# Raw weights in one ring of six blocks, and another order of the Strassen groups in two runs of a Trainium2 kernel

## The chip, the cores and the metric

The kernel runs on one core of a Trainium2 chip. Five engines with instruction queues of their own work side by side: TensorE (PE, with its weight loads shown apart as PEld), VectorE (DVE), ScalarE (ACT), GpSimd (POOL) and SyncE (SP), whose queue issues most of the DMAs. An instruction starts when those before it on its engine have been issued and the semaphores that it waits for have been raised. The metric is the time of one execution on the device in microseconds (us); lower is better.

## What is computed

Attention with sigmoid weights for 2 batches of 12 heads (448 positions, 64 wide), then a gated MLP behind an RMS norm, then a second MLP, all in FP32 on 896 tokens (cut from the reference):

```
scores = scale * matmul(q, k.T) - log(S)
x = matmul(1 / (1 + exp(-scores)), v)                    # as 896 tokens x 768
xn = x / sqrt(mean(x * x) + 1e-6) * rms_g
h = silu(xn @ w_gate) * (xn @ w_val)                     # 768 -> 1536
y = h @ w_out                                            # 1536 -> 768
h2 = y @ w_in                                            # 768 -> 2048
return (h2 * sigmoid(h2)) @ w_out2                       # 2048 -> 768
```

## The kernel before

**Products.** An FP32 product is three passes of rounded operands (high by high, high by low, low by high). Most matrix products are Strassen runs: seven groups of matmuls on 2x2 blocks, named by the weight side A11, S1, S2, A12, S3, S4 and A22, each 128x128 against 128x448 columns, collecting in PSUM banks x, y, z (L798). Plain products are on L747. ACT *saves* a bank between groups where one bank is used for several (L830, L884, tiles named ..s0 to ..s3), and DVE adds the rest (L836, L891, L978, L1062, L1065). The stages in order of time: attention, g and v (the gated MLP), o0 to o2 (its output, "the layer behind the norm"), i0 to i7 (in the second MLP), e0, e1, e2, e0b, e1b (its output).

**Weights.** They come as 76 slabs of 64-bit words, 52 of 768 KB (six tiles of 128 columns) and 24 of 512 KB (four tiles, the short slabs of the o stages and of some in e). One SP DMA loads a slab into a raw buffer (L239). ACT takes the exponent part out of it (L257, into a buffer named f, or `spare` for single tiles) and turns the other half in place (L265), DVE merges both (L269). Sums and differences of blocks are made in place (L687 to L709), and each *piece* that a group needs is split into a high part on ACT (L245) and a low part on DVE (L248) in a ring of nine. `wraw` is a pool of two buffers of a full slab each, so two slabs are in flight at most, whatever their width.

**What sets the order.** A class `Plan` holds every operation as a job with its engine, cost, dependencies and, where needed, a stock that it takes ("raw", "f", "ring", "alt", "sum"). PE's jobs stand in program order; the others get a due time, counted back from their users by cost, a factor WAIT, an engine's LAG and HOP, and each engine takes the startable job that is due first. That simulated order is what the engines' queues hold. A load is a job of SP that takes "raw", given back by the merge, and counts with LAG["S"] = 4.4 us.

**The o stages.** `mixed` does o0 and o1 with `ahead=True`: first the plain products of the two-bank pairs a and b (o0a, o0b), then the groups in the order A11, S1, S2, A12, S3, S4, A22. Before the groups, ACT saves bank b's first half (tile s3); A11, S2, S3 and A22 go to bank x, S1 and S4 to y, A12 into bank a. Bank pair b is free for the next stage after that save and the addition c11, which follows S3.

Of the kernel before, what the change touches and what calls it, by code (L numbers as in the profile page):

```python
# [22 lines left out]
P = 128  # L23
# [16 lines left out]
LAG = {"A": 0.0481, "D": 0.081, "P": 0.165, "S": 4.4, "G": 5.0}  # L40
HOP = {"A": 0.516, "D": 0.3833, "S": 0.4, "G": 0.5}
# [34 lines left out]
class Plan:  # L76
# [37 lines left out]
    def run(self, busy):  # L114
# [8 lines left out]
        for j in reversed(self.jobs):  # L123
            if j.eng != "P":
                j.due = min([u.due for u in j.users + j.users_of_gift], default=1e9) - WAIT[j.eng] * j.cost - LAG[j.eng] - HOP[j.eng]
# [30 lines left out]
        while left:  # L156
# [6 lines left out]
            while again:  # L163
                again = False
                for e in ("P", "D", "A", "S", "G"):
# [17 lines left out]
                    end = now + j.cost + LAG[e]  # L183
# [14 lines left out]
def tile_attention_two_mlps(  # L198
# [12 lines left out]
    wraw = ctx.enter_context(tc.tile_pool(name="wraw", bufs=2))  # L211
# [23 lines left out]

    def load(s):
        raws[s] = wraw.tile([P, 2 * SLAB], U32, tag="raw", name=f"raw{s}")
        n = 2 * wide(s)
        nc.sync.dma_start(raws[s][:, :n], wd[s].bitcast(U32)[:, :n])  # L239

    def load_next():
        load(order.pop(0))
# [7 lines left out]
    def words(s):  # L250
        return raws[s][:, : 2 * wide(s)].rearrange("p (n two) -> p n two", two=2)
# [329 lines left out]
    plan = Plan({"raw": 0, "f": 1, "ring": RING - 8, "alt": 1, "sum": 1, "ps": 0, "one": 0})  # L581
# [57 lines left out]
    wjob = {}  # L639
# [21 lines left out]
    def weight_mac(macs, act_z, alt=True, early=False):  # L661

        todo = [mac_steps(s, n, act_z, alt, early) for s, n in macs]
        for _ in range(8):
            for t in todo:
                next(t)

    def mac_steps(s, n, act_z, alt, early):
# [24 lines left out]

        s1 = dve(hw, first, m, take=None if inside else "sum")
# [24 lines left out]
        if one:  # L719
            plan.frees("alt" if alt else "f", l1, l2, l4, l5, l6)  # L720
        else:
            if not inside:
                plan.frees("sum", l1, s2)
            plan.frees("f", *[l2, l5] + ([l1] if inside else []))
            plan.frees("alt" if inside else "f", l4, l6)
# [146 lines left out]
    def mixed(  # L872
# [26 lines left out]
        if ahead:  # L899
            bx, by = Banks(f"{name}x"), Banks(f"{name}y")  # L900
            ba, bb = Banks(f"{name}a", True), Banks(f"{name}b", True)
            bz, bv, bu, bw = ba.bank(0), ba.bank(1), bb.bank(0), bb.bank(1)
            done = []
            for k in range(0, n, 2):
                for m, t in enumerate((ba, bb)):
                    i = 2 * k + 2 * m
                    done += product(
                        [t.bank(0), t.bank(1)], w[i : i + 2], keys[k : k + 2], (0, 1), first=k == 0,
                        final=k == n - 2 and m > 0, take="ps" if k == 0 else None, start=t.start if k == 0 else None,
                    )  # L910
            u = save(3, bu, done[-1])
        else:
            bx, by, bz, bw = (Banks(f"{name}{c}") for c in "xyzw")
# [6 lines left out]
        g4 = g(bz, "A12", start=not ahead, stop=ahead, first=None if ahead else bz)  # L920
        if ahead:
            a00 = add(0, bz, [g4, v0], 0, 0)
        g5 = g(bx, "S3", deps=[v2])
        a11 = add(1, bx, [g5, v1])
        if ahead:
            c11 = add(1, bw, [a11], 1, 1)
            bb.read_by(u, c11)
        g6 = g(by, "S4", stop=ahead, deps=[v1])
        if ahead:
            a01 = add(2, by, [g6, v2])  # L930
            c01 = add(2, bv, [a01], 0, 1)
            by.read_by(v1, a01)
            ba.read_by(a00, c01)
        if not ahead:
            p0 = product([bz, by], w[:n], keys, (0, 1), first=False)
        g7 = g(bx, "A22", stop=ahead, deps=[a11])
        if ahead:
            a10 = add(3, bx, [g7, u], 1, 0)
            bx.read_by(a10)
            return  # L940
# [442 lines left out]
    for t in range(3):  # L1383
        dest = lambda m, b, t=t: r2[t]()[:, b, m]
        n = 0 if t < 2 else 3
        macs, plain = [(s + 2, 3), (s + 4, 1)] if t < 2 else [(s, 3), (s + 2, 1)], s + n
# [4 lines left out]
        if t < 2:  # L1391
            weight_mac(macs, ZO)
        macs = [(macs[0][0], range(3)), (macs[1][0], (3,))]
# [184 lines left out]
```

## Time and profile before

| | |
|---|---|
| median of 3 runs | 523.17 us (521.27 to 523.77) |
| profiled execution | 522.38 us |
| its span, first to last instruction | 520.4 us |
| PE busy | 515.3 us (99%) |
| DVE busy | 471.3 us (91%) |
| ACT busy | 380.5 us (73%) |
| granted TensorE clock | 1.00 of full |
| moved by DMA | 70.5 MB |

The profiled execution takes 2.0 us outside the span of its instructions. Busy time is by the hardware's records; matmuls are pipelined, so one's record overlaps the next.

### The profile page before, as it was taken

The page shows a single profiled execution, that of the slowest core. Times are in us where ns is not written, and L with a number is a line of the kernel's source. Part 1 is how long each engine was busy: PE and PEld are TensorE (multiplying, and loading weights), DVE is VectorE, ACT ScalarE, POOL GpSimd, SP SyncE. Part 2 cuts the span into 40 slices and gives each one's busy share as a digit, 9 for nine tenths or more (in the row PEclk, how much of TensorE's full clock was granted, in tenths as well). Part 3 has the DMA queues.
Part 4 walks back from the last instruction along what each step waited for, and adds up shares of the span by engine and source line. Part 5 has one row for each costly group of instructions (what it writes and reads, how often), then busy time and mean ns, then how long its engine had stood idle before and what let it go on. Part 6 is the DMA issues. An engine that isn't in the chain of part 4 may idle for free.

```text
span 520.4 us, 7479 instructions
## 1 busy us (share of the span) xinstructions
PE 515.3 (99%) x2654; PEld 442.7 (85%) x2654; DVE 471.3 (91%) x883; ACT 380.5 (73%) x677; POOL 13.5 (3%) x28
## 2 busy tenths in 40 slices
PE   9999999999999999999999999999999999999996
PEld 4444469999999999999999999999998999999996
DVE  6799999999999888799989989999988899999992
ACT  6876754787888676876777868998888887778730
POOL 0000000000000000000000000000010101111000
PEclk9999999999999999999999999999999999999999
DMA  8774111033332353411442362333355242555531
GB/s 319 276 248 162 62 62 60 1 122 122 121 123 88 103 209 108 162 42 40 163 161 82 125 217 84 122 121 123 135 186 195 97 134 95 169 199 200 187 123 71
DMA packets 18116, 70.51 MB, mean 136 GB/s; under 512 B 2464, under 2 KB 5024, under 8 KB 18080
## 3 DMA queue, kind: packets, MB, share of 16 engines
q1 hardware_dynamic: 16400, 64.32, 35.8%
q0 software_dynamic: 1536, 5.51, 3.1%
q8 instruction: 20, 0.33, 0.3%
q10 hardware_dynamic: 144, 0.23, 0.1%
q14 instruction: 16, 0.13, 0.1%
HBM read 64.54 MB, written 5.51 MB: 135 GB/s over the span
## 4 chain that ended last, share of the span: by engine, by line
PE 99%; DVE 0%; issue 0%
PE av L409 7%; PE sc L382 6%; PE g L747 3%; PE e2S L798 3%; PE v L747 3%; PE e1x L798 2%; PE o2x L798 2%; PE o1x L798 2%; PE e0bx L798 2%; PE o0x L798 2%; PE e2a L798 2%; PE i6x L798 1%; PE g2x L798 1%; PE i7x L798 1%; PE e0x L798 1%; PE e1bx L798 1%
## 5 line engine op out<-in xcount | busy, mean ns | idle before, releaser
L265 ACT ACTIVATE raw<-raw 128x768 int32<-128x768 uint32 (+1 forms) x70 | 57.4, 825 | 12.9 <-DMA raw<-in_w 9.4
L269 DVE SCALAR_TENSOR_TENSOR f<-f,raw 128x768 uint32<-128x768 uint32 (+1 forms) x65 | 58.4, 900 | 7.5 <-ACT f L257 5.9
L245 ACT ACTIVATE w_S<-f 128x384 fp32r<-128x384 f32 (+1 forms) x90 | 44.7, 497 | 23.0 <-DVE f L698 7.7
L257 ACT ACTIVATE f<-raw 128x768 f32<-128x768 f32 (+1 forms) x65 | 55.7, 859 | 4.4 <-DVE w_S L248 2.6
L248 DVE TENSOR_TENSOR w_S<-f,w_S 128x384 fp32r<-128x384 f32 (+1 forms) x90 | 47.3, 526 | 4.7 <-ACT w_S L245 4.3
L391 ACT ACTIVATE a<-sc,logs 128x896 f32<-128x896 f32 x42 | 39.1, 1008 | 15.3 <-PE sc L382 15.3
L245 ACT ACTIVATE w_A<-f 128x384 fp32r<-128x384 f32 (+1 forms) x84 | 41.2, 500 | 7.2 <-PE o2y L747 1.8
L248 DVE TENSOR_TENSOR w_A<-f,w_A 128x384 fp32r<-128x384 f32 (+1 forms) x84 | 43.8, 533 | 1.8 <-ACT w_A L245 1.8
L409 PE MATMUL av<-a,vr 128*64 128x448 f32 (+1 forms) x192 | 35.4, 552 | 0.0
L409 PEld LDWEIGHTS av<-a,vr 128*64 128x64 f32 (+1 forms) x192 | 10.4, 135 | 21.3 <-issue 20.3
L382 PEld LDWEIGHTS sc<-ks 64*128 64x128 f32 x204 | 18.3, 186 | 10.5 <-issue 5.5
L382 PE MATMUL sc<-ks 64*128 64x448 f32 x204 | 24.7, 380 | 0.0
L1131 DVE TENSOR_TENSOR g<-g 128x448 f32<-128x448 f32 x32 | 19.4, 620 | 0.1
L245 ACT ACTIVATE w_S<-s 128x384 fp32r<-128x384 f32 x24 | 12.5, 520 | 6.0 <-PE g L747 3.1
L709 DVE TENSOR_TENSOR f<-f 128x384 f32<-128x384 f32 (+1 forms) x30 | 15.8, 525 | 0.2
L245 ACT ACTIVATE w_A<-spare 128x128 fp32r<-128x128 f32 (+1 forms) x21 | 7.0, 334 | 12.0 <-DVE spare L269 8.7
L747 PE MATMUL v<-x,w 128*128 128x448 f32 x72 | 15.3, 370 | 0.0
L747 PE MATMUL g<-x,w 128*128 128x448 f32 x72 | 15.3, 368 | 0.0
L747 PEld LDWEIGHTS g<-x,w 128*128 128x128 f32 x72 | 13.4, 188 | 1.7 <-issue 0.7
L747 PEld LDWEIGHTS v<-x,w 128*128 128x128 f32 x72 | 13.5, 188 | 1.4 <-issue 0.4
L248 DVE TENSOR_TENSOR w_S<-s,w_S 128x384 fp32r<-128x384 f32 x24 | 13.3, 552 | 0.9 <-ACT w_S L245 0.9
L687 DVE TENSOR_TENSOR s<-f 128x384 f32<-128x384 f32 x24 | 13.3, 554 | 0.3
(1462 smaller groups left out, 1506.3 us busy)
## 6 DMA issues: line engine op xcount, KB each, us to landing
raw<-in_w SPq DMA_DIRECT2D x52, 768.0 KB, 4.4
raw<-in_w SPq DMA_DIRECT2D x24, 512.0 KB, 3.5
kq<-in_kq SPq DMA_DIRECT2D x11, 448.0 KB, 5.5
out_t<-e SPq DMA_DIRECT2D x8, 224.0 KB, 1.9
vr<-in_v SPq DMA_DIRECT2D x6, 256.0 KB, 4.5
vr<-in_v SPq DMA_DIRECT2D x6, 192.0 KB, 2.5
g_4away<-g POOLq DMA_DIRECT2D x4, 224.0 KB, 2.5
g<-g_4away POOLq DMA_DIRECT2D x4, 224.0 KB, 2.9
```

The source lines that it names most:

```text
L245: nc.scalar.activation(dst, src, AF.Copy)
L248: nc.vector.tensor_tensor(dst, src, hi.bitcast(F32), ALU.subtract)
L257: nc.scalar.activation(floats[s], words(s)[:, :, 1].bitcast(F32), AF.Prelu, scale=2.0**-112, alpha=2.0**32)
L265: nc.scalar.activation(z.bitcast(I32), z, AF.Copy, scale=2.0**-29 * (1 - 2.0**-18), bias=-0.5 + 2.9e-5)
L269: nc.vector.scalar_tensor_tensor(fu, fu, 3, words(s)[:, :, 0], ALU.logical_shift_left, ALU.bitwise_or)
L382: nc.tensor.matmul(ps[to, h, :S], k_[:, keys], q_, start=(step == 0), stop=(step == 2 or plain), skip_group_check=True,)
L391: nc.scalar.activation(a, ps[:, :, :S], AF.Sigmoid, bias=logs, scale=D**-0.5)
L409: nc.tensor.matmul(av[n][h * D : (h + 1) * D, :S], vr[i][rows, c, h, :], a[rows, h, :], start=(begun[n] == 1), stop=(begun[n] == KC + 1), ...
L709: s4 = dve(hw, lambda: tt(block(1), block(1), block(0), ALU.subtract), [s2, l3])
L747: nc.tensor.matmul(banks[b](), t[:, jw], act[key](jx, b), start=(first and i == 0 and n_ == 0), stop=(final and i == n - 1 and n_ == 2), s ...
L798: nc.tensor.matmul(ps(), w[:, jw, j * P : (j + 1) * P], book[t][USES[a]][jx], start=(start and i == 0 and n == 0), stop=(stop and i == len ...
L1131: sub = lambda d, a, b: (lambda: tt(d(), a(), b(), ALU.subtract))
```

## The change

The two buffers of `wraw` become one tile `store` of the same size, seen as six blocks. `place(s)` gives slab s the next three blocks (six tiles) or two (four tiles) in the order in which the program names the slabs, and wraps to block 0 where the rest doesn't suffice; it returns the slabs that held those blocks. The load no longer takes "raw": it depends on the merges of these slabs. The lag of a load depends on its width now (2.6 + 0.45 per tile: 5.3 us for six tiles and 4.4 us for four).

In o0 and o1 the groups run in the order A11, A12, S4, S1, S2, A22, S3; S4 collects in the second half of bank a, A22 in the first half of bank b, and tile s3 is saved from bank x behind S3, at the end. `raw_steps` makes the pieces in the matching order, and the single-tile slab of these stages is listed ahead of the two six-tile ones. The number of computing instructions of each kind stays.

```diff
+    store = wraw.tile([P, 4 * SLAB], U32, name="raw")
+    owner, end = [None] * 6, [0]
+    def place(s):
+        n = 2 * wide(s)
+        at = end[0] if end[0] + n <= 4 * SLAB else 0
+        raws[s], end[0] = store[:, at : at + n], at + n
+        over = {}
+        for k in range(at // (4 * P), (at + n) // (4 * P)):
+            over[owner[k]] = True
+            owner[k] = s
+        return over
...
-        r = None if s in LOADED else plan.add("S", 0.4, lambda: load(s), take="raw")
+        over = [] if s in LOADED else place(s)
+        r = None if s in LOADED else plan.add("S", 0.4, lambda: load(s), [merged[u] for u in over if u is not None])
+        if r:
+            r.lag = LOAD + LOAD_TILE * tiles
...
-        return plan.frees("raw", dve(n, lambda: merge(s), [e, z]))
+        merged[s] = dve(n, lambda: merge(s), [e, z])
+        return merged[s]
...
-            u = save(3, bu, done[-1])
+            v0 = save(0, bx, g(bx, "A11", start=True, stop=True, first=bx))
+            a00 = add(0, bz, [g(bz, "A12", stop=True), v0], 0, 0)
+            g6 = g(bv, "S4", stop=True)
+            g2_ = g(by, "S1", start=True, stop=True, first=by)
+            v1 = save(1, by, g2_)
+            g3 = g(bx, "S2", deps=[v0])
+            v2 = save(2, bx, g3)
+            a01 = add(2, by, [g2_, v2])
+            by.read_by(v1, a01)
+            c01 = add(2, bv, [a01, g6], 0, 1)
+            ba.read_by(a00, c01)
+            g7 = g(bu, "A22", stop=True)
+            g5 = g(bx, "S3", deps=[v2], stop=True)
+            a11 = add(1, bx, [g5, v1])
+            c11 = add(1, bw, [a11], 1, 1)
+            v3 = save(3, bx, g5)
+            a10 = add(3, bu, [g7, v3], 1, 0)
+            bx.read_by(a11, v3)
+            bb.read_by(c11, a10)
+            return
...
-        macs, plain = [(s + 2, 3), (s + 4, 1)] if t < 2 else [(s, 3), (s + 2, 1)], s + n
+        macs, plain = [(s + 4, 1), (s + 2, 3)] if t < 2 else [(s, 3), (s + 2, 1)], s + n
```

PE, the first groups of o0, before. A row is output<-activation,weight piece; w26 is the wide pair of slabs, w28 the single tile.

```order
L798 MATMUL o0x_2402<-x2l1_1101,w26_A11_2261 128x448 x3
L798 MATMUL o0x_2402<-h1B11_1398,w26_A11_2261 128x448 x3
L798 MATMUL o0x_2402<-h1tl0_1625,w26_A11_2261 128x448 x3
L798 MATMUL o0x_2402<-lone_850,w28_A11_2384 128x448 x3
L798 MATMUL o0y_2427<-x4_87,w26_S1_2387 128x448
```

The same place after:

```order
L848 MATMUL o0x_2373<-x5_89,w28_A11_2231 128x448 x3
L848 MATMUL o0a_2291<-x0_84,w26_A12_2303 128x448 x3
L848 MATMUL o0a_2291<-h1B21_1412,w26_A12_2303 128x448 x3
L848 MATMUL o0a_2291<-lone_843,w26_A12_2303 128x448 x3
L848 MATMUL o0a_2291<-x2l0_1065,w28_A12_2301 128x448 x3
L848 MATMUL o0a_2291<-x2_86,w26_S4_2402 128x448 x3
L848 MATMUL o0a_2291<-h1B21_1412,w26_S4_2402 128x448 x3
L848 MATMUL o0a_2291<-x1h0_1040,w26_S4_2402 128x448 x3
L848 MATMUL o0a_2291<-x2l1_1093,w28_S4_2400 128x448 x3
L848 MATMUL o0y_2447<-x4_88,w26_S1_2417 128x448
```

A12 and S4 moved ahead of S1, two groups of 12 matmuls; S3 now ends the stage.

ACT, the passage from o0 to o1, before. f31, f32 and raw31 are the wide pair of o1, yr0 the result of o0.

```order
L257 ACTIVATE f31_2553<-raw31_2493 128x768 [waits DMAHW2_49,Activation_49]
L265 ACTIVATE raw31_2493<-raw31_2493 128x768
L245 ACTIVATE y1_1_2569<-yr0_2515 128x448 [waits DVE_49]
L245 ACTIVATE w31_A11_2588<-f31_2553 128x384 [waits DVE_49,PE_49]
L257 ACTIVATE f32_2592<-raw32_2539 128x768 [waits DMAHW3_49,Activation_49]
```

The same place after:

```order
L934 ACTIVATE o0s3_2554<-o0x_2373 128x448 [waits DVE_49]
L261 ACTIVATE y1_1_2565<-yr0_2519 128x448 [waits DVE_49]
L273 ACTIVATE f31_2575<-raw_79 128x768 [waits DMAHW3_49,Activation_49]
L281 ACTIVATE raw_79<-raw_79 128x768
L273 ACTIVATE f32_2585<-raw_79 128x768 [waits DMAHW4_49,Activation_49]
L281 ACTIVATE raw_79<-raw_79 128x768
L261 ACTIVATE y1_1_2565<-yr0_2519 128x448 [waits DVE_49]
L261 ACTIVATE w31_A11_2604<-f31_2575 128x384 [waits DVE_49,PE_49]
```

The save of bank x stands in front of all work on o1's wide slabs, and both slabs are now prepared before the first piece of them.

SP, the last loads, before. The last raw load is slab 75, the second half of the weights of e1b.

```order
L239 DMA raw73_4782<-in_w 128x1024 [waits DMAHW2_49,DVE_49]
L239 DMA raw74_4856<-in_w 128x1536 [waits DMAHW3_49,DVE_49]
L239 DMA raw75_4892<-in_w 128x1536 [waits DMAHW4_49,DVE_49]
L1461 DMA out_t<-e2s1_4858 128x448 [waits DVE_49]
L1461 DMA out_t<-e2s0_4818 128x448 [waits DVE_49]
```

The same place after:

```order
L253 DMA raw_79<-in_w 128x1536 [waits DMAHW3_49,DVE_49,Activation_49]
L1514 DMA out_t<-e2s0_4750 128x448 [waits DVE_49]
L1514 DMA out_t<-e2s1_4755 128x448 [waits DVE_49]
L1514 DMA out_t<-e2s3_4825 128x448 [waits DVE_49]
L253 DMA raw_79<-in_w 128x1536 [waits DMAHW5_49,DMAHW4_49,DVE_49]
L1514 DMA out_t<-e2s2_4791 128x448 [waits DVE_49]
```

The load of slab 75 moved behind three stores of results and waits for DVE's merge of slab 74, whose blocks it takes.

DVE, from the merge of slab 75 to the first piece that needs it, before:

```order
L269 SCALAR_TENSOR_TENSOR f75_5006<-f75_5006,raw75_4892 128x768 [waits DMAHW6_49,Activation_49]
L1065 TENSOR_TENSOR e2s3_4878<-e2a_4588,e2s3_4878 128x448
L687 TENSOR_TENSOR s74_5029<-f75_5006 128x384 [waits DVE_49]
L978 TENSOR_TENSOR e0_4826<-e0bx_4898,e0_4826 128x448 [waits PE_49]
L695 TENSOR_TENSOR f75_5006<-f74_4918,f75_5006 128x384 [waits DVE_49]
L1065 TENSOR_TENSOR e2s2_4854<-e2b_4625,e2s2_4854 128x448
L698 TENSOR_TENSOR f74_4918<-s74_5029,f74_4918 128x384 [waits DVE_49]
L248 TENSOR_TENSOR w74_S1_5036<-s74_5029,w74_S1_5036 128x384 [waits Activation_49]
L978 TENSOR_TENSOR e0_4826<-e0by_4928,e0_4826 128x448 [waits PE_49]
```

The same place after:

```order
L1031 TENSOR_TENSOR e0_4753<-e0bx_4829,e0_4753 128x448 [waits PE_49]
L285 SCALAR_TENSOR_TENSOR f75_4949<-f75_4949,raw_79 128x768 [waits DMAHW1_49,DVE_49,Activation_49]
L707 TENSOR_TENSOR s74_4970<-f75_4949 128x384 [waits DVE_49]
L1031 TENSOR_TENSOR e0_4753<-e0by_4852,e0_4753 128x448 [waits PE_49]
L728 TENSOR_TENSOR f75_4949<-f74_4849,f75_4949 128x384 [waits DVE_49]
L731 TENSOR_TENSOR f74_4849<-s74_4970,f74_4849 128x384 [waits DVE_49]
L264 TENSOR_TENSOR w74_S1_4979<-s74_4970,w74_S1_4979 128x384 [waits Activation_49]
```

The addition of bank e0by, which waits for a group of PE, moved from behind the first piece of slab 75 to ahead of it.

## Rows read from the trace of the kernel before

**Rows 1.** The page: span, busy time per engine, chain that ended last.

```profile
span 520.4 us, 7479 instructions
...
PE 515.3 (99%) x2654; PEld 442.7 (85%) x2654; DVE 471.3 (91%) x883; ACT 380.5 (73%) x677; POOL 13.5 (3%) x28
...
PE 99%; DVE 0%; issue 0%
```

**Rows 2.** Windows: stretch, length, busy per engine (count), PEclk, DMA share, GB/s.

```profile
102.00:230.00 128.00, 127.98 (x632) 118.30 (x631) 116.66 (x208) 99.28 (x177) 0.00 (x0) 1.00 0.35 122
230.00:284.00 54.00, 54.00 (x269) 50.04 (x268) 51.21 (x108) 37.10 (x77) 0.00 (x0) 1.00 0.32 108
284.00:480.00 196.00, 196.00 (x965) 180.79 (x964) 182.76 (x349) 158.38 (x301) 11.91 (x22) 1.00 0.43 146
```

**Rows 3.** Waits of PEld, 102 to 521 us: us in total, times, longest.

```profile
PEld g2x L798 <- ACT g2s L830: 0.4, 1, 0.4
PEld i6x L798 <- ACT i6s L830: 0.3, 1, 0.3
```

**Rows 4.** Timeline of PE in o1: start, length, line, output<-inputs, shapes, count.

```profile
256.82 1.78 PE L747 MATMUL o1a<-x,w 128*128 128x448 f32 x8
...
259.25 0.36 PE L747 MATMUL o1b<-x,w 128*128 128x448 f32 x1
...
266.55 0.77 PE L798 MATMUL o1x<-x2l,w_A 128*128 128x448 f32 x3
```

**Rows 5.** Timeline of ACT, the late save of i6.

```profile
389.38 1.40 ACT L865 ACTIVATE g<-g 128x896 f32<-128x896 f32 x2
390.69 0.52 ACT L830 ACTIVATE i6s<-i6x 128x448 f32<-128x448 f32 x1
```

**Rows 6.** Timeline of ACT ahead of the late save of g2.

```profile
129.67 0.91 ACT L265 ACTIVATE raw<-raw 128x768 int32<-128x768 uint32 x1 [2.20 <-DMA raw<-in_w]
130.47 0.52 ACT L245 ACTIVATE w_S<-f 128x384 fp32r<-128x384 f32 x1
```

**Rows 7.** The page's groups: busy, mean ns of one | idle before.

```profile
L265 ACT ACTIVATE raw<-raw 128x768 int32<-128x768 uint32 (+1 forms) x70 | 57.4, 825 | 12.9 <-DMA raw<-in_w 9.4
L269 DVE SCALAR_TENSOR_TENSOR f<-f,raw 128x768 uint32<-128x768 uint32 (+1 forms) x65 | 58.4, 900 | 7.5 <-ACT f L257 5.9
...
L257 ACT ACTIVATE f<-raw 128x768 f32<-128x768 f32 (+1 forms) x65 | 55.7, 859 | 4.4 <-DVE w_S L248 2.6
```

**Rows 8.** The page's DMA issues: count, KB each, median us to landing.

```profile
raw<-in_w SPq DMA_DIRECT2D x52, 768.0 KB, 4.4
```

**Rows 9.** The tile raw over the whole span: what a landing took.

```profile
DMA to landing us min/median/max: 3.3/4.3/6.7
```

**Rows 10.** Timeline of DVE, the passage from o0 to o1.

```profile
257.13 0.62 DVE L891 TENSOR_TENSOR yr<-o0x,o0s 128x448 f32<-128x448 f32 x1
257.67 0.55 DVE L248 TENSOR_TENSOR w_A<-f,w_A 128x384 fp32r<-128x384 f32 x1
```

**Rows 11.** Timeline of DVE, slabs 73 to 75: low pieces, a merge, an addition.

```profile
489.96 0.28 DVE L248 TENSOR_TENSOR w_S<-spare,w_S 128x128 fp32r<-128x128 f32 x1
490.16 0.96 DVE L269 SCALAR_TENSOR_TENSOR f<-f,raw 128x768 uint32<-128x768 uint32 x1
491.03 0.56 DVE L248 TENSOR_TENSOR w_A<-f,w_A 128x384 fp32r<-128x384 f32 x1
...
500.85 0.56 DVE L248 TENSOR_TENSOR w_S<-s,w_S 128x384 fp32r<-128x384 f32 x1
501.31 0.62 DVE L978 TENSOR_TENSOR e<-e0by,e 128x448 f32<-128x448 f32 x1
```

**Rows 12.** Timeline of PE, first matmuls on the pieces of Rows 11.

```profile
492.91 0.37 PE L798 MATMUL e0bx<-x,w_S 128*128 128x448 f32 x1
...
493.52 0.77 PE L798 MATMUL e0bz<-g4B,w_A 128*128 128x448 f32 x3
...
505.07 0.37 PE L798 MATMUL e1by<-x,w_S 128*128 128x448 f32 x1
```

More of the change, by code (lines that the diff above doesn't have):

```diff
@@ L234, in wide @@
         return short.get(s, SLAB)
+    store = wraw.tile([P, 4 * SLAB], U32, name="raw")
[9 more added lines that the diff above has]
+        return over
     def load(s):
-        raws[s] = wraw.tile([P, 2 * SLAB], U32, tag="raw", name=f"raw{s}")
-        n = 2 * wide(s)
-        nc.sync.dma_start(raws[s][:, :n], wd[s].bitcast(U32)[:, :n])
+        nc.sync.dma_start(raws[s], wd[s].bitcast(U32)[:, : 2 * wide(s)])
     def load_next():
-        load(order.pop(0))
+        s = order.pop(0)
+        place(s)
+        load(s)
     def high(dst, src):
@@ L579, in tile_attention_two_mlps @@
     pools = {"T": tp, "F": fp, "x": xp, "r": rp, "e": ep}
-    plan = Plan({"raw": 0, "f": 1, "ring": RING - 8, "alt": 1, "sum": 1, "ps": 0, "one": 0})
+    plan = Plan({"f": 1, "ring": RING - 8, "alt": 1, "sum": 1, "ps": 0, "one": 0})
     tt = nc.vector.tensor_tensor
@@ L718, in mac_steps, with raw_steps @@
         l6 = made("A22", lambda: block(3), [m[1]])
[L719 to L725, printed above, removed]
+        frees(l1, l2, l4, l5, l6, s2)
+        yield
+    def raw_steps(s, n, act_z, alt, early):
+        hw, one, inside, m, sums, block, first, made, frees = mac_blocks(s, n, act_z, alt, early)
+        s1 = dve(hw, first, m, take=None if inside else "sum")
+        s3 = dve(hw, lambda: tt(block(2), block(0), block(2), ALU.subtract), [s1, m[0]])
+        yield
+        l0 = made("A11", lambda: block(0), [m[0]])
+        s2 = dve(hw, lambda: tt(block(0), sums[0], block(0), ALU.subtract), [s3, l0])
+        yield
+        l3 = made("A12", lambda: block(1), [m[0]])
+        s4 = dve(hw, lambda: tt(block(1), block(1), block(0), ALU.subtract), [s2, l3])
+        yield
+        l5 = made("S4", lambda: block(1), [s4])
+        yield
+        l1 = made("S1", lambda: sums[0], [s1])
+        yield
+        l2 = made("S2", lambda: block(0), [s2])
+        yield
+        l6 = made("A22", lambda: block(3), [m[1]])
+        yield
+        l4 = made("S3", lambda: block(2), [s3])
+        frees(l1, l2, l4, l5, l6, s2)
         yield
@@ L919, in mixed @@
         v2 = save(2, bx, g3)
-        g4 = g(bz, "A12", start=not ahead, stop=ahead, first=None if ahead else bz)
-        if ahead:
-            a00 = add(0, bz, [g4, v0], 0, 0)
+        g(bz, "A12", start=True, first=bz)
         g5 = g(bx, "S3", deps=[v2])
         a11 = add(1, bx, [g5, v1])
[L925 to L940, printed above, removed]
+        g(by, "S4", deps=[v1])
+        p0 = product([bz, by], w[:n], keys, (0, 1), first=False)
+        g(bx, "A22", deps=[a11])
         a00 = add(0, bz, [p0[-1], v0], 0, 0)
```

36 lines of the change are left out of this document (24 added, 12 removed).

## The prediction

> **What bounds the kernel now.** I read the page's engine line and chain first, then windows by stage, then the waits of PE's weight loads, and last the timelines of ACT and DVE where something was late. PE is busy 515.3 of 520.4 us, and the chain that ended last is PE for 99% of the span [rows 1]. Busy time alone could mislead, since a matmul's record (0.36 us) overlaps the next. So look at starts: from the first matmul of o1a at 256.82 to the first of o1b at 259.25 twelve matmuls take 2.43 us, 0.203 us from start to start [rows 4]. The windows show the same without a gap: 127.98 of 128, 54.00 of 54 and 196.00 of 196 us, at the full granted clock, which is the upper of the two levels, 2.4 GHz [rows 2]. Behind 102 us only two waits of the weight loads are listed, 0.4 us for a save in g2 and 0.3 us for one in i6 [rows 3]. DVE is nearly as busy (91%), but nothing waits for it in those rows.
>
> So the time is a count of matmuls times 0.203 us. The change leaves the count alone. What earlier weights can give back behind 102 us is 0.4 + 0.3 = 0.7 us, and neither wait is for weights.
>
> **The change, part by part.**
>
> *The ring of six blocks.* It costs no instruction. Three short slabs can be under way where two were, in the o stages and where four-tile slabs meet in e; two long slabs fill the ring as two buffers did. The load's landing is 4.4 us for a long slab [rows 8], 3.3 to 6.7 over all [rows 9]. In o0 PE doesn't wait for anything [rows 2], so loads that start earlier there make pieces that lie longer: 0 us. If that cover were absent, nothing else in the span would show a wait for a piece either [rows 3].
>
> *The new order of the groups in o0 and o1.* Same matmuls, same additions and saves; 0 us on PE as long as three chains hold.
>
> First, bank pair b. Its last reader is now an addition at the end of o0: S3 ends about 0.2 us behind 256.82; then an addition on bank x (0.62, the size of [rows 10]), the save of the same bank on ACT (0.52, the size of [rows 5]) and the last addition (0.62): 257.0 + 0.62 + 0.52 + 0.62 = 258.8. With three hops between engines, estimated at 0.1 together, 258.9. o1b starts at 259.25 [rows 4]. It holds by 0.35 us; one addition more in front on DVE makes it late by 0.27. I take 0, with 0 and 0.6 as ends.
>
> Second, o1's first wide pieces. On ACT's queue the save above stands in front, and it waits for S3 and for DVE; behind it stand a cast and the two preparations of both wide slabs. From 258.2: a cast (0.52, the nearest row), two exponents (0.86 each) and two halves in place (0.83 each) [rows 7] give 262.1; DVE's merge (0.90), one sum and the low part (0.55 each, as [rows 10]) give 264.1. PE wants them at 266.55 [rows 4]: a lead of 2.4 us, where before the low part ended at 258.22, 8.3 us ahead [rows 4, 10]. No loss, but a cover of 6 us is spent.
>
> Third, the last groups of each stage win cover, since their pieces are made in the same sequence: nothing was waiting there, so 0.
>
> *The new due times.* Lags and dependencies change the simulated clock of the planner, so ACT's and DVE's rows differ from about g1 on. PE's don't until o0. Here two things can be priced. The save of i6 stood behind two silu halves of 1.40 us [rows 5] and is moved out from behind them: minus 0.3 [rows 3]. The save of g2 stands behind a half in place and a high piece as before (0.91 and 0.52 [rows 6]): its 0.4 stays. About as many saves as before get a new long neighbour on ACT. Between a plain run's first group and its third lie nine matmuls, 1.83 us; less the save's 0.52 and about 0.2 of hops, 1.1 us may stand in front of it. One neighbour of 0.9 fits; two don't. I take one new wait of 0.3 as likely as none, and 0 to 3 as ends: 0.0 to 0.9 us.
>
> *The end.* Slab 75's load now waits on SP behind three stores, and for the merge of slab 74, whose blocks it takes. Before, that merge ran from 490.16 to 491.12 [rows 11]; with an addition more in front it ends by 491.7. Landing 4.4 later, 496.1 (498.4 at the longest of [rows 9]); exponent and half in place 0.86 + 0.83, merge 0.90, sum 0.55: 499.2 (501.5). Then on DVE comes the addition on bank e0by, which ran at 501.31 because PE ends its group there [rows 11]; behind it two differences and the low part, 0.62 + 3 x 0.56 from 501.31 (501.5): 503.6 (503.8). PE wants it at 505.07 [rows 12]: a lead of 1.3 to 1.5 us, where before it was 505.07 - 501.41 = 3.7 [rows 11, 12]. 0 us.
>
> *The pieces of e0b.* Two result additions of e2 and the merge of slab 74 now stand ahead of the single tile's S2 piece on DVE, two additions more ahead of the wide A12 piece. Issued every 0.53 and 0.87 us, as the neighbours of [rows 11] are, that is 1.9 and 1.1 us. The leads were 492.91 - 490.24 = 2.7 and 493.52 - 491.59 = 1.9 us [rows 11, 12]; about 0.8 is left in both. This is the tightest place that the change makes. 0 taken, 0 and 0.8 as ends.
>
> *Sum.* 522.38 (profiled) - 0.3 (i6) + 0.3 x 1/2 (new saves) = about 522.2 for a profiled run. The median of the three runs is 523.17, 0.8 above the profiled one, and a median is what will be compared: 522.2 + 0.8 = 523.0; I say 522.9.
>
> **The rivals.** A: as above, 522.9, no place where PE waits longer than a few tenths; its own range 521.7 to 524.2, from the spread of the runs (521.27 to 523.77) and 0.9 us of saves.
> B: every wait behind 102 us goes: 523.17 - 0.7 = 522.5. For it: both are of ACT's order, which changes. Against it: g2's neighbours stay.
> C: the change doesn't do what it says: long slabs still go in pairs, short ones land earlier and lie. 523.2. Half of it is true in any case.
> D, slower: saves behind two long ACT instructions. Price 0.3 to 0.4 each [rows 3], and there are 34 first-or-third-group saves of bank x in the seventeen plain runs. It decides from eight new ones; ten give 523.2 + 3.5 = 526.7. For it: ACT is 73% busy with 0.8 to 0.9 us instructions [rows 1, 7]. Against: only 2 of 34 were late before, with as many long neighbours.
> E, slower: the spent cover runs out, at o1's first piece (2.4 us), e0b (0.8) or the last slab (1.3). A landing of 6.7 instead of 4.4 in o1 takes 2.3 of its 2.4 us; with one merge (0.90) more in front it is late by 0.8. The same merge more at e0b makes it late by 0.1. Together 0.9, so 524.1; past 525.8 only if a whole preparation of two slabs (3.4) is late.
> F, much faster: each 0.203 us hides a wait on the weights that the ring removes, and a matmul in o0 and o1 goes as fast as its weight load, 50.04 / 268 = 0.187 us [rows 2]. In those 54 us that is 269 x 0.016 = 4.3 us: 518.9. Against it: full windows at a DMA share from 0.32 to 0.43 alike [rows 2]; a wait on weights would vary from stage to stage.
> The Trainium skill (TensorE: Matmul & The Clock Gate, section "Wait — 56ns, not 53.3ns?") gives N ÷ 2.4 GHz plus about 2.5 ns from start to start: 189 ns for 448 columns, so 14 ns of each matmul would be to be had, 3.8 us in these stages and a time of 519.4. The trace shows 0.203 us at the full clock [rows 2, 4] and no row at 0.189; I go by the trace.
>
> **How the numbers follow.** Chances: A 0.70, B 0.08, C 0.08, D 0.05, E 0.06, F 0.03. About 0.5%, 2.6 us, is what a measurement of this kernel can tell from no change: below 520.6 or above 525.8. Faster is F: 0.03, and 0.01 for a low median; slower is D, and half of E's harsher end with the upper tail of A, 0.05: 0.10; the same is the rest, 0.86. The range leaves out D, F and the far ends of A and E: 521.3 (B with the lowest run's 1.2 below) to 524.9 (E at 524.1 with 0.8 of spread).
>
> **What would show it.** PE's windows stay full (54.00 of 54) and start to start stays 0.203; the list of PE's weight-load waits has no i6 row, still the g2 row, and zero to three new ones named by a save. o1b's first matmul follows o1a's without a wait on DVE; o1's A11 pieces end some 2 us ahead of PE instead of 8; the last raw load issues near 491.7. Wrong would be: a wait for a low part (L248 of before) at o1's A11, e0b's S2 or A12, or e1b's S1; a wait of the weight loads on DVE's addition at o1b; or a median past 525.8.

## The result

The changed kernel takes 526.66 us (median of 6, 525.68 to 528.74), the kernel before 522.39 us in the same comparison (median of 6, 521.27 to 523.77). The ratio is 1.0082, 95% interval 1.0062 to 1.0103: slower by 0.8%. The prediction was 522.9 with a range that ended at 524.9; the result lies 1.8 us above that end.

The page of the kernel after, for [rows 1]: span, TensorE, and the chain that ended last.

```profile
span 523.9 us, 7450 instructions
...
PE 515.1 (98%) x2654; PEld 442.3 (84%) x2654; DVE 470.3 (90%) x883; ACT 381.6 (73%) x677; POOL 13.5 (3%) x28
...
PE 83%; DVE 9%; issue 3%; ACT 2%; DMA 2%; POOL 0%; DVEq 0%; ACTq 0%
```

The work is the same (2654 matmuls, 515.1 us), but the chain is PE for 83% where it was 99%: it now runs through DVE and ACT in places. The windows of [rows 2] and the list of the weight loads' waits behind 102 us, [rows 3], say where. After, windows (stretch, length, then busy time and count per engine: PE, PEld, DVE, ACT, POOL):

```profile
102.00:230.00 128.00, 128.00 (x633) 118.65 (x632) 114.68 (x208) 99.44 (x179) 0.00 (x0) 1.00 0.35 120
230.00:284.00 54.00, 53.28 (x264) 49.06 (x263) 49.99 (x103) 37.34 (x75) 0.00 (x0) 1.00 0.36 122
284.00:480.00 196.00, 193.67 (x951) 178.22 (x950) 180.00 (x348) 157.16 (x297) 11.68 (x21) 1.00 0.42 140
```

After, waits of PEld from 102 us to the end (us in total, times, longest):

```profile
PEld e0x L848 <- ACT e0s L1024: 2.7, 1, 2.7
PEld o1a L848 <- DVE yr L941: 1.1, 1, 1.1
PEld e2S L848 <- DVE w_S L264: 0.9, 1, 0.9
```

Both waits of before (g2, i6) are gone; three others have come, in o1, e0 and e2. Measured on PE's starts, beyond the usual distance of two matmuls, they cost 0.98, 2.60 and 0.80 us. The first matmul of some stages, us from the span's start:

| | g1 | o0 | i0 | e0 | e1 | e2 | e0b | PE's end |
|---|---|---|---|---|---|---|---|---|
| before | 102.09 | 230.07 | 310.32 | 413.69 | 430.90 | 452.18 | 486.23 | 516.18 |
| after | 101.16 | 228.84 | 310.08 | 412.83 | 432.55 | 454.25 | 489.65 | 519.60 |
| after - before | -0.93 | -1.23 | -0.24 | -0.86 | 1.65 | 2.07 | 3.42 | 3.42 |

Up to o0 the kernel after was 1.2 us ahead: 0.9 from the attention stage, 0.3 from the wait in g2 that is gone. Neither is shown to come from the change: g1 begins at 101.16 in one execution of after and at 102.61 in another (after_look2), and in a second execution of before (before_look2) it begins at 101.57 and g2 has no listed wait either. After lost 1.0 in o1, won 0.6 in i, lost 2.5 in e0, 0.4 in e1 and 1.35 in e2. e2's loss is 0.80 of wait; the rest there and in e1, and part of i's gain, is a change of PE's pace, told under the four single executions.

**o1.** PE and DVE at the wait, after (start, length, line, output<-inputs, shapes, count, idle time before and what ended it):

```profile
271.40 0.77 PE L848 MATMUL o1a<-x1h,w_S 128*128 128x448 f32 x3
272.88 0.88 PE L848 MATMUL o1a<-x2l,w_S 128*128 128x448 f32 x3 [0.72 <-DVE yr L941]
```

```profile
272.20 0.62 DVE L941 TENSOR_TENSOR yr<-o1a,o1s 128x448 f32<-128x448 f32 x1 [1.87 <-PE o1a L848]
272.75 0.55 DVE L264 TENSOR_TENSOR w_S<-f,w_S 128x384 fp32r<-128x384 f32 x1
```

The change lets S4 collect in the second half of the two-bank tile o1a whose first half holds A12. The addition that reads A12's half stands on DVE in the middle of S4. It waits 1.87 us for the ninth matmul of S4, which writes the *other* half; S4's tenth then waits until the addition has read. Each waits for the other in turn, though they touch different halves. In o0 the addition comes after S4, and nothing waits.

**e0.** PE stands for the save of bank x; ACT has it behind two casts of one activation, g4B, which POOL fetches back from DRAM. PE after, ACT after:

```profile
427.49 0.47 PE L848 MATMUL e0x<-x,w_S 128*128 128x448 f32 x1 [2.33 <-ACT e0s L1024]
```

```profile
421.25 0.57 ACT L261 ACTIVATE x<-g 128x448 fp32r<-128x448 f32 x1
425.40 1.04 ACT L261 ACTIVATE g4B<-g 128x448 fp32r<-128x448 f32 x2 [3.58 <-DMA g<-g_4away]
426.35 0.66 ACT L273 ACTIVATE f<-raw 128x512 f32<-128x512 f32 x1
426.91 0.52 ACT L1024 ACTIVATE e0s<-e0x 128x448 f32<-128x448 f32 x1
```

ACT idles 3.58 us at the casts, and the save, whose group had ended on PE, is behind them and one instruction of a slab's preparation. POOL's four transfers of that activation, 224 KB each, go one after another. After (the first two and the last of four), then before (first and last):

```profile
409.75 0.55 POOL L1290 DMA_DIRECT2D g<-g_4away  x1 [23.10 <-PE i7x L848]
415.72 0.56 POOL L1290 DMA_DIRECT2D g<-g_4away  x1 [5.42 <-issue]
...
421.99 0.56 POOL L1290 DMA_DIRECT2D g<-g_4away  x1 [2.54 <-issue]
```

```profile
409.29 0.55 POOL L1237 DMA_DIRECT2D g<-g_4away  x1 [21.80 <-PE i7x L798]
...
419.08 0.56 POOL L1237 DMA_DIRECT2D g<-g_4away  x1 [2.61 <-issue]
```

The first transfer took 5.67 us instead of 3.15; the last landed at 425.38 instead of 421.91. The ring has a part in that. Slab 58 is short and takes blocks 0 and 1, slab 59 takes 2 to 4, so slab 60 wraps to 0 to 2 and has to wait for the merge of slab 59, its direct predecessor, which runs on DVE from 408.10 to 409.05. Its load goes at 409.08, 0.4 us ahead of the load of slab 61, where before it went at 399.77 and slab 61 alone at 407.77. SP, after and before:

```profile
409.08 0.80 SPq L253 DMA_DIRECT2D raw<-in_w  x2
```

```profile
407.77 0.33 SPq L239 DMA_DIRECT2D raw<-in_w  x1
```

Before, the casts stood ahead of two saves as well (ACT before, the casts and the second save):

```profile
421.93 1.05 ACT L245 ACTIVATE g4B<-g 128x448 fp32r<-128x448 f32 x2 [1.03 <-DMA g<-g_4away]
...
424.48 0.53 ACT L971 ACTIVATE e0s<-e0x 128x448 f32<-128x448 f32 x1
```

There the save of bank x ended at 425.01 and PE came to its next group there at 426.03: 1.0 us of slack. After, the save ended at 427.43, 2.4 later, while PE was 1.0 earlier: 2.4 + 1.0 - 1.0 = 2.4 us of wait, of the 2.60 measured. In before_look2 the first of the two saves held PE for 0.26 us behind the same casts: the place was narrow before the change.

**e2.** PE after; DVE after; then the windows of before and after around this place:

```profile
482.97 0.37 PE L848 MATMUL e2S<-g7tl,w_S 128*128 128x448 f32 x1
483.87 0.47 PE L848 MATMUL e2S<-lone,w_S 128*128 128x448 f32 x1 [0.53 <-DVE w_S L264]
```

```profile
482.38 1.10 DVE L264 TENSOR_TENSOR g7tl<-g,x 128x896 fp32r<-128x896 f32 x1
483.39 0.43 DVE L264 TENSOR_TENSOR w_S<-f,w_S 128x256 fp32r<-128x256 f32 x1
```

```profile
466.00:484.00 18.00, 18.00 (x90) 16.68 (x89) 17.94 (x37) 14.27 (x27) 2.75 (x5) 1.00 0.63 205
```

```profile
466.00:484.00 18.00, 17.47 (x85) 15.53 (x85) 17.94 (x36) 12.52 (x23) 2.45 (x5) 1.00 0.55 180
```

DVE has no gap before the late piece: from 466 to 484 us it is busy 17.94 of 18, as it was before. It has no reserve there in which to catch up. That the 3.2 us which it idled at the g4B casts come out here is a guess, and save_first below speaks against it.

Of the twelve executions of one kernel below, order_nowait, two, the profiled one among them, took 529.0 and 529.3 us and the others 520.8 to 523.6; its ratio leaves the two out.

### The profile page after: what moved, and what is told of

Read it like the earlier page. It is cut to its first block, busy times and chain, and to the rows that moved or that the text cites. A ratio compares the mean times of both kernels' runs of the same rounds, so it can differ in the third digit from the quotient of the medians.

```text
span 523.9 us, 7450 instructions
## 1 busy us (share of the span) xinstructions
PE 515.1 (98%) x2654; PEld 442.3 (84%) x2654; DVE 470.3 (90%) x883; ACT 381.6 (73%) x677; POOL 13.5 (3%) x28
## 4 chain that ended last, share of the span: by engine, by line
PE 83%; DVE 9%; issue 3%; ACT 2%; DMA 2%; POOL 0%; DVEq 0%; ACTq 0%
PE av L425 6%; PE sc L398 6%; PE v L797 3%; PE g L797 2%; PE e0bx L848 2%; PE o2x L848 2%; PE e1bx L848 1%; PE i5x L848 1%; PE g3x L848 1%; PE v5x L848 1%; PE i6x L848 1%; PE i2x L848 1%; PE i1x L848 1%; PE o0x L848 1%; PE g5x L848 1%
## 5 line engine op out<-in xcount | busy, mean ns | idle before, releaser
L742 DVE TENSOR_TENSOR f<-f 128x384 f32<-128x384 f32 (+1 forms) x28 | 14.7, 525 | 0.1
L264 DVE TENSOR_TENSOR ks<-kq,ks 128x896 fp32r<-128x896 f32 (+2 forms) x14 | 13.2, 949 | 0.4
```

What stands on the lines that cost most here:

```text
L264: nc.vector.tensor_tensor(dst, src, hi.bitcast(F32), ALU.subtract)
L742: s4 = dve(hw, lambda: tt(block(1), block(1), block(0), ALU.subtract), [s2, l3])
```

## The experiments

Three theories stood after the traces. One: the wait in o1 is the shared two-bank tile and belongs to the new order. Two: the wait in e0 is the ring's wrap (late loads go beside POOL's transfers). Three: the wait in e0 is ACT's order, casts that wait for a DMA ahead of saves. All times are medians; the kernel before had 522.52 in the first four comparisons, 522.68 in the next three and in fixed, and 522.81 beside the four single executions.

**ring_only**: the ring and the loads' lag of the change, with groups and pieces in the order of before; mixed and weight_mac are those of before (the diff is against after).

```diff
-            weight_mac(macs, ZO, raw_first=True)
-        macs = [(w, range(3) if n == 3 else (3,)) for w, n in sorted(macs)]
+            weight_mac(macs, ZO)
+        macs = [(macs[0][0], range(3)), (macs[1][0], (3,))]
...
```

> The changed kernel with the groups and pieces of o0 and o1 in the old order: only the ring of six blocks and the load's lag by width are new. The changed kernel is 4.3 us above the one before (526.66 against 522.39), and its trace shows three waits of PE: 1.0 us in o1, 2.6 in e0, 0.8 in e2. Theory (the ring's wrap makes e0's wait, the e0 wait makes DVE late for e2, the new order makes o1's): no wait in o1, 2 to 3 us in e0 and 0.5 to 1 in e2, 525.6 us (525.0 to 526.4). Rival 1 (the new order of the groups is behind most of it, the planner's later rows follow from it): no wait in e0, 522.4 to 523.0. Rival 2 (each new plan of ACT and DVE costs some waits anywhere): waits at other places, 523 to 526.

Measured: 525.55 us (524.74 to 529.17), ratio 1.0060 (1.0039 to 1.0082). The first waits of PEld:

```profile
PEld e2S L818 <- DVE w_S L264: 1.9, 2, 1.2
PEld e0x L818 <- ACT e0s L991: 1.5, 1, 1.5
PEld o0y L818 <- DVE h2th L264: 1.0, 1, 1.0
...
```

The ring with its lag brings the losses in e0 (1.43 us on PE's starts) and e2 (1.76), and none in o1. It also brings a series of small waits in o0, some 2.0 us together, for low parts of activations on DVE. After doesn't have these: there A12 and S4, 24 matmuls, stand between A11 and the groups S1 and S2 that need those parts. So the new order does hide something that the ring's plan makes late. The ring was not run with the old lag of 4.4 us for every load, nor the new lag without the ring: how the two share these losses stays open.

**order_only**: the new order with the two buffers of before; mixed, raw_steps and weight_mac are those of after, the loads those of before (the diff is against before).

```diff
-            u = save(3, bu, done[-1])
...
+            g6 = g(bv, "S4", stop=True)
...
-        macs, plain = [(s + 2, 3), (s + 4, 1)] if t < 2 else [(s, 3), (s + 2, 1)], s + n
+        macs, plain = [(s + 4, 1), (s + 2, 3)] if t < 2 else [(s, 3), (s + 2, 1)], s + n
```

> The kernel before with the new order of groups and pieces in o0 and o1 alone; raw buffers, their stock and the lag as before. Theory: one wait of 0.7 to 1.1 us in o1, inside the S4 group, none in e0 and e2: 522.4 + 1.0 - 0.0 to 0.5 = 523.2 us (522.7 to 523.8). Rival 1: 525.5 to 526.7, with waits in e0. Rival 2: no wait in o1, some elsewhere.

Measured: 525.31 us (522.17 to 526.63), ratio 1.0037 (1.0015 to 1.0059). In the trace one wait is left behind 102 us, 1.06 us on PE's starts:

```profile
PEld o1a L828 <- DVE yr L921: 1.2, 1, 1.2
```

The wait in o1 is the new order's; e0's and e2's come with the ring and its lag. But one wait of 1.06 us doesn't make a profiled run of 526.52 us: that is taken up below, with two more executions of the same kernel.

**s1_first**: after, with group S1 and its piece ahead of S4.

```diff
-            g6 = g(bv, "S4", stop=True)
             g2_ = g(by, "S1", start=True, stop=True, first=by)
+            g6 = g(bv, "S4", stop=True)
```

> The changed kernel with S1 ahead of S4 in o0 and o1 (A11, A12, S1, S4, S2, A22, S3), so that twelve matmuls (2.4 us) lie between the last matmul into the first half of bank pair a and the first into its second half. Theory: o1's wait of 1.0 us is gone, e0 and e2 as in the changed kernel: 525.6 us (525.0 to 526.4). Rival (o1's S4 waits for its weight piece, not for the addition that reads the other half): the wait stays at about 1 us and 526.7.

Measured: 530.05 us (529.39 to 532.23), ratio 1.0138 (1.0108 to 1.0168). The wait in o1 is gone, and o0 has one in its place, at S4, 1.45 us, for the same addition (PE; DVE):

```profile
247.56 0.85 PE L848 MATMUL o0a<-x,w_S 128*128 128x448 f32 x3 [1.21 <-DVE yr L941]
```

```profile
246.80 0.62 DVE L941 TENSOR_TENSOR yr<-o0a,o0s 128x448 f32<-128x448 f32 x1
```

That speaks for the shared tile: S4 waits for the reader of A12's half where DVE comes to it late. As a cure it fails: e0 (2.04) and e2 (2.07) lose 4.1 us together, where after loses 3.4, and in the profiled execution PE goes at the slower of two paces (below) from 248 to 431 us, some 890 matmuls or 3.6 us.

**aligned**: after, with long slabs only at block 0 or block 3, so that none takes blocks of the slab just ahead of it.

```diff
-        at = end[0] if end[0] + n <= 4 * SLAB else 0
+        at = -(-end[0] // (2 * SLAB)) * 2 * SLAB if n == 2 * SLAB else end[0]
+        at = at if at + n <= 4 * SLAB else 0
```

> The changed kernel with long slabs placed at block 0 or 3 only, so that none lies across the middle: slab 60's load waits for slab 58's merge and not for slab 59's. Theory: that load goes some 8 us earlier, no longer together with slab 61's and against the return of tile g2_4; the e0 wait of 2.6 falls below 0.3, and with it the one of e2 below 0.3; o1 keeps 1.0: 526.7 - 3.2 = 523.5 us (522.9 to 524.0). Rival 3 (the casts that wait for the return stand ahead of the save whatever the transfers do): e0 keeps 1 us or more, 524.5 to 526.5. Rival 4 (e2's wait has its own cause): e2 keeps 0.8, 524.2.

Measured: 524.02 us (523.27 to 526.12), ratio 1.0024 (1.0007 to 1.0041). Waits, and ACT where PE stands in e0:

```profile
PEld e0y L849 <- ACT e0s L1025: 2.1, 1, 2.1
PEld o1a L849 <- DVE yr L942: 1.1, 1, 1.1
```

```profile
423.77 0.58 ACT L262 ACTIVATE g4B<-g 128x448 fp32r<-128x448 f32 x1 [2.79 <-DMA g<-g_4away]
424.25 0.53 ACT L1025 ACTIVATE e0s<-e0y 128x448 f32<-128x448 f32 x1
```

Slab 60's load now goes at 405.50 (3.6 us earlier than in after, not the 8 expected) and slab 61's at 411.80; the first return takes 2.81 us, and the last lands at 423.74, 1.6 earlier than in after. Still PE loses 2.0 us, at another save behind the first cast. A save that stands behind a cast which waits for a DMA holds PE without the wrap, too. How much of after's 2.60 is the wrap's this run can't tell, since its plan also changes ACT's order: the first cast now stands ahead of the save of bank y. The wait in e2 is gone here. Of the 2.6 us between the medians of after and aligned (other comparisons), the profiled executions account for 0.6 in e0, 0.8 in e2 and 1.1 of pace.

**save_first**: after, with the casts of g4B held behind e0's second and third save.

```diff
+            for c in casts:
+                for v in (v1, v2):
+                    c.deps.append(v)
+                    v.users.append(c)
...
+            if q == 4:
+                casts.append(h_)
```

> The changed kernel with one edit: ACT's casts of tile g2_4, which wait for POOL's return of that tile, are queued behind e0's second and third saves. Theory 2 (the casts in front of the save make e0's wait, the late DVE behind them e2's): slab 60 and 61 still load together near 409 us and the last return lands near 425 as in the changed kernel, but PE's waits of 2.6 us in e0 and 0.8 in e2 fall below 0.3 each; o1 keeps 1.0. Rival (the transfers themselves hold PE): e0 keeps over 1.5. Second theory, on the pace: behind a wait PE goes on at 0.2027 or at 0.2067 us from matmul to matmul until the next wait; so behind o1's wait the some 1250 matmuls left cost 0 or up to 5.0 us more, and runs spread from 523 to 528 us, wider than the kernel before without its slow runs.

Measured: 524.25 us (523.50 to 526.72), ratio 1.0034 (1.0017 to 1.0052). Waits; POOL behind the first return; ACT, the save and the casts:

```profile
PEld e2S L848 <- DVE w_S L264: 1.9, 2, 1.2
PEld o1a L848 <- DVE yr L941: 1.1, 1, 1.1
```

```profile
416.78 0.56 POOL L1299 DMA_DIRECT2D g<-g_4away  x1 [5.32 <-issue]
```

```profile
423.92 0.55 ACT L1024 ACTIVATE e0s<-e0x 128x448 f32<-128x448 f32 x1
...
426.60 1.05 ACT L261 ACTIVATE g4B<-g 128x448 fp32r<-128x448 f32 x2 [1.68 <-DMA g<-g_4away]
```

e0's wait is gone, with the wrap still in place, the longest return still 5.6 us and the last landing at 426.58, later than in after. So the transfers don't hold PE by themselves: theory three, the order on ACT, is what lets them. Theory two still has its part, since before had the casts ahead of the saves too and, with the last landing 3.5 us earlier than in after, no wait there in its profiled execution. e2 was expected below 0.3 and got worse (0.80 to 1.75), though DVE idles only 1.3 us at the casts here, so its wait isn't a mere consequence of what e0 loses.

**order_nowait**: order_only, with the addition of A12's half queued behind S4.

```diff
-            a00 = add(0, bz, [g(bz, "A12", stop=True), v0], 0, 0)
+            g4 = g(bz, "A12", stop=True)
             g6 = g(bv, "S4", stop=True)
+            a00 = add(0, bz, [g4, g6, v0], 0, 0)
```

> The kernel before with the new order in o0 and o1 (as order_only, 525.3 us) and one edit: the addition that reads the first half of bank pair a is queued behind the S4 group. Theory 2: the wait of 1.06 us inside o1's S4 is gone. Pace theory: with no wait left from 102 us to the end PE stays at 0.2027 us all the way, and the time falls by more than the wait: 521.3 to 522.3 us, a gain of 3 to 4 on order_only, with runs within 1 us. Rival (a wait costs its length and nothing else): 525.3 - 1.1 = 524.2.

Measured: 522.43 us (520.84 to 529.30), ratio 0.9992 (0.9976 to 1.0007). No wait of PE behind 102 us is listed. Theory one holds: with the addition behind S4 the shared tile costs nothing, and the new order alone is as fast as before. The gain on order_only is 2.9 us by the medians (other comparisons), for a wait of 1.06; by the means of all twelve executions each it is 1.6.

The expectation on the pace didn't hold. In the profiled execution (529.30 us) PE goes at 0.2067 us from 131 us to the end, with 428 matmuls here:

```profile
300.00:388.00 88.00, 88.00 (x428) 79.93 (x427) 82.10 (x149) 72.86 (x132) 1.23 (x2) 1.00 0.40 137
```

That pace began at a weight load of g2 that came 0.1 us late, too little for the list; some 1890 matmuls at 0.004 us are 7.6 us.

**pool_fixed**: after with that same edit, and the planner counting POOL's transfers of this activation at 3.15 us each with a lag of 0.1, as they ran, instead of 1.2 and 5.0.

```diff
-LAG = {"A": 0.0481, "D": 0.081, "P": 0.165, "S": 4.4, "G": 5.0}
+LAG = {"A": 0.0481, "D": 0.081, "P": 0.165, "S": 4.4, "G": 0.1}
-            gone = [plan.add("G", 1.2, out_(m, b), [j]) for j, m, b in parts]
+            gone = [plan.add("G", 3.15, out_(m, b), [j]) for j, m, b in parts]
-                    jobs.append(plan.add("G", 1.2, back(m, b), gone, need=ready))
+                    jobs.append(plan.add("G", 3.15, back(m, b), gone, need=ready))
```

> The changed kernel with the planner told what a transfer of POOL takes (3.15 us one after the other in place of 1.2 each and 5.0 us to landing), and with the addition in o1 behind S4. The ring stays as it is. Theory 2: no wait of PE over 0.3 us behind 102 us, pace 0.2027 throughout: 521.3 to 522.5 us, equal to or just below the kernel before (522.5). Rival (the ring's wrap costs time by itself): e0 or e1 keep 1 us or more, 524 and up.

Measured: 525.16 us (524.92 to 526.04), ratio 1.0049 (1.0032 to 1.0066). No wait in o1 or e0, 0.25 in e2, but a loss of 3.8 us in e0b (PE; DVE; window behind the wait, PEclk the third number from its end):

```profile
491.73 1.16 PE L848 MATMUL e0bx<-g4th,w_S 128*128 128x448 f32 x3 [1.99 <-DVE e L1032]
```

```profile
490.96 0.62 DVE L1032 TENSOR_TENSOR e<-e0bx,e 128x448 f32<-128x448 f32 x1
```

```profile
492.10:495.40 3.30, 3.30 (x11) 2.92 (x10) 2.37 (x6) 1.42 (x4) 0.00 (x0) 0.50 0.83 235
```

Of the 3.8 us 2.2 are the wait. Behind it the granted clock is at its lower level, 0.50 of full or 1.2 GHz, for 3.4 us, and the matmuls start 0.37 us apart; that is the other 1.6.

True prices for four transfers cure the place where they stand and, by way of the whole plan, hurt the next: e0b's addition is now behind five result additions of e2 and a merge. The planner's price of these transfers let the casts stand ahead of the saves; the cure has to leave the rest of the order alone.

**fixed**: aligned, save_first and order_nowait's edit together.

> The changed kernel with long slabs at block 0 or 3, the casts of g2_4 behind e0's saves and the addition in o1 behind S4: all three causes taken away. Theory 2 and pace: 521.3 to 522.3 us, no wait over 0.3, 0.2027 throughout. If a wait appears at another place, the planner's new rows made it: then 522.5 to 526 by its length and the pace behind it.

Measured: 521.83 us (521.25 to 522.75), ratio 0.9984 (0.9970 to 0.9998).

```profile
PEld e2S L849 <- DVE w_S L265: 0.5, 1, 0.5
```

One wait is left, 0.41 us on PE's starts, and from it to the end PE goes at 0.2067 us, where no wait over 0.3 and 0.2027 throughout were expected. By the medians it is 4.8 us faster than after (of another comparison), and its gain on before, 0.2%, is at the edge of what a measurement tells. So the two causes, with the placement, were worth the whole loss, and the idea of the change without them little more than nothing. The two edits without the placement were not run, so what the placement adds to them stays open.

**Four single executions** of kernels that were there already: order_look2 and order_look3 are order_only, after_look2 is after, before_look2 is before.

> The same kernel as order_only, one more look. There PE went on at 0.2067 us from its wait in o1 (271 us) to the end, where it had gone at 0.2027 up to it. If the pace behind a wait is drawn anew in every execution, this look may show 0.2027 behind the same wait, and then a time lower by up to 1250 x 0.004 = 5.0 us: 521.5 to 522.5 us at the fast pace throughout, near 526.5 at the slow one. Rival (the kernel's order fixes the pace): 0.2067 from the same matmul, 526 to 527 us.

> As order_look2, a third look at the same kernel: either pace behind the wait of o1, and a time that follows from it.

> The changed kernel, one more look. The three waits (o1 1.0, e0 2.6, e2 0.8 us) are there again within 0.3 us each, since they come from its order; what differs from the first look (525.68 us, 0.2067 from 429 to 485 us only) is where PE goes at 0.2067: 525 to 529 us by that. Rival: other waits, or these by other amounts.

> The kernel before, one more look. Its two short waits (0.4 us in g2, 0.3 in i6) are there again; behind each the pace is 0.2027 or 0.2067: 521 to 524 us, higher only if the slow pace starts at g2 already. Rival (the pace belongs to the kernel's order): 0.2067 from 391 to 424 us and 0.2027 elsewhere, as in the first look.

Measured: order_look2 525.61, order_look3 523.17, after_look2 528.82, before_look2 521.73 us. The same kernel, order_only, in one stretch without a wait, in two executions, the profile of order_only and that of order_look3:

```profile
300.00:388.00 88.00, 88.00 (x428) 79.91 (x427) 82.15 (x148) 73.05 (x131) 1.78 (x3) 1.00 0.42 141
```

```profile
300.00:388.00 88.00, 88.00 (x435) 81.29 (x434) 82.33 (x149) 72.64 (x132) 1.77 (x3) 1.00 0.42 142
```

Both are full, both have the full granted clock, and one does 428 matmuls where the other does 435. In the traces a matmul starts 0.2027 or 0.2067 us after the one before, as a mean over some dozens at the full clock; nothing lies between for long. The pace changes where PE has waited, if only some 0.06 us for a weight load, and then stays but for a few steps. order_only kept the slow one from its wait at 272 us to the end; order_look2, with the same wait (1.05) and one in i6 (0.8 in the list), from 393 only; order_look3, with 1.05 in o1 and 1.3 in i6, not at all. About 1210 matmuls at 0.004 us are 4.9 us; less the waits in i and g2 that order_look3 has and order_only has not (1.6), 3.3 are left, and the profiled runs differ by 3.35. After had the slow pace from 428 to 484 us, after_look2 from 487 on; before from 391 to 424, before_look2 nowhere.

after_look2 had waits at the same three places as after, 0.99, 2.48 and 1.27 us on PE's starts, e2's 0.5 longer. What makes it 3.1 us longer than after is mostly something else: the attention stage ends 1.45 us later, and behind e0's wait the granted clock is at its lower level for 3.4 us, which costs 1.5:

```profile
430.00:433.00 3.00, 3.00 (x10) 2.69 (x9) 3.00 (x7) 2.53 (x5) 0.00 (x0) 0.50 0.93 318
```

In after PE does 17 matmuls in the same window, at the full clock, behind a wait of 2.60. before_look2 had no wait listed in g2, 0.77 us in i6 and 0.26 in e0.

## Why the prediction was wrong

It counted 522.2 for a profiled run; the profiled run of after took 525.68. The step that failed is the price of PE's waits: 0 for the ring, 0 for the new order of the groups, and 0.15 for new saves, where the trace has 0.98 us in o1, 2.60 in e0 and 0.80 in e2. The largest part is a save on ACT behind casts that wait for a DMA, which no term and no rival had. By its steps:

- **What bounds the kernel.** "*Count of matmuls times 0.203 us*" was right for most of the span and left out that PE has a second pace. The trace of before held it: from 391 to 424 us, behind the wait in i6. In the profiled pair this is worth 0.65 us on one side and about 1.0 on the other, so it isn't the cause of the loss there. The pace, and the lower clock level behind two of the longer waits, are ways in which a wait costs more than its length in some executions.
- **"*Nothing waits for DVE*"** was true of before, and no reserve: DVE was busy 17.94 of 18 us from 466 to 484 us in before too. A piece that came late there cost 0.80 us in e2. No term stood for it.
- **The ring, 0 us.** "*Two long slabs fill the ring as two buffers did*" holds for a row of long slabs only; across a short one a later long slab takes blocks of its direct predecessor. The load of slab 60 went 9.3 us later than before and beside the next one, and g4B's last part landed 3.5 us later. In ring_only the ring with its lag has 1.43 us of wait in e0, 1.76 in e2 and 2.0 in o0, and a median 3.0 us above before.
- **The first chain of the new order.** Bank pair b held, as worked out: DVE's last addition on it ends at 257.68 and o1b starts at 258.03, with no wait and the 0.35 us that were counted. Bank pair a was not looked at. A12 and S4 share its tile, and that is the 0.98 us of o1; in order_nowait, the new order alone, one line undoes it.
- **The second and third chain**: o1's first wide pieces came without a wait, and no wait came at the last groups of o0 and o1. In o0 the new order even hides some 2 us, which ring_only shows.
- **The due times.** The i6 wait went, as said (in other executions of before and order_only it is there, 0.8 to 1.3 us, so its size differs from run to run). The g2 wait went too, where 0.4 was to stay, but before_look2 doesn't have it either. For new waits of saves 0.15 was taken and 0.9 was the bound; one came and cost 2.60. This is the term with the largest miss. Bound and rival D looked for saves behind two long ACT *instructions*; it was a save behind a cast that stands still 3.58 us for a DMA. The idle column of [rows 6] shows the form (2.20 us at a load); the casts of g4B were not followed to POOL, though they stood ahead of two saves in before with 1.0 us to spare.
- **The end, and the pieces of e0b**: no wait in after, as said. The last load went at 495.54 where 491.7 was said, with the program 3.4 us behind there, and PE still didn't wait. The narrow place was there: in pool_fixed e0b lost 3.8 us. (The 0.53 us from one addition to the next is near the 0.54 of [rows 10]; [rows 11] has no such step.)
- **The rivals.** D had the side (slower) with chance 0.05 and the wrong mechanism, many short waits where three came; that its 526.7 meets the median is chance. E's three places all held. F, the wait hidden in each matmul, found nothing: no run shows a pace below 0.2027 us. The Trainium skill (TensorE: Matmul & The Clock Gate, "Wait — 56ns, not 53.3ns?") leads to an estimate of 189 ns, and the two paces here, 202.7 and 206.7 ns, both speak against that for these pairs of a weight load and a matmul.
- **The sum, as it was**: 522.38 + 4.38 (three waits) - 0.48 (g2 and i6) + 0.4 (pace) - 0.93 (attention ends earlier) = 525.75; measured 525.68. The median lies 1.0 above that run, the lowest of its six; the early end of its attention stage, which after_look2 doesn't share, was luck. The 0.8 us that the prediction added for the median rested on three executions; the median of six of before is 522.39.

What stays open: what makes PE take the slow pace behind one wait and not behind another; why the granted clock fell behind a wait of 2.2 us in pool_fixed and 2.5 in after_look2 and not behind 2.6 in after; how the ring and the new lag share the losses; and why e2's piece is late by 0.80 in after, 1.75 in save_first and not at all in aligned. That DVE is full there is shown; which of the moved instructions makes the difference isn't.

## What to carry to other kernels

A ring of blocks with two sizes of entries isn't the two buffers that it replaces: follow the placement through every change of size and ask whose end each load waits for. On an engine that works in order, look for instructions that wait for a DMA, not only for long ones, and for what stands behind them; where a planner orders the work, compare its price of that transfer with the trace. And where two accumulations come to share one tile, check its readers too: the wait of 1 us that this made went with medians 2.9 us apart.

## What the hardware showed

TensorE went at either of two paces, 0.2027 or 0.2067 us from start to start, at full granted clock in both; the pace changed at a wait, if only of a weight load, and differed between executions of one kernel. In before itself, PE, at the slow pace and then, in the next groups but one, at the fast:

```profile
421.13 0.37 PE L798 MATMUL e0x<-g0th,w_S 128*128 128x448 f32 x1
...
423.40 0.37 PE L798 MATMUL e0x<-lone,w_S 128*128 128x448 f32 x1
...
426.03 0.37 PE L798 MATMUL e0x<-g0th,w_S 128*128 128x448 f32 x1
...
427.86 0.36 PE L798 MATMUL e0x<-x,w_S 128*128 128x448 f32 x1
```

Eleven steps take 2.27 us (0.206), nine take 1.83 us (0.203). In after_look2 and pool_fixed the granted clock went to its lower level for 3.4 us behind waits of 2.5 and 2.2 us, with matmuls 0.37 us apart. POOL's four transfers of 224 KB went one after another, 2.8 to 3.2 us each in before, and one that met two loads of 512 and 768 KB took 5.67 in after.
